# Block attention and a two-level Strassen feed-forward on one core: second-level weight sums one step later, two first loads on GpSimd's queue, a fifth raw weight tile, idle matmuls in two more places

## The chip, the core and the metric

One NeuronCore of a Trainium2 chip runs the whole program. Its engines work side by side and each runs its own instructions in order: TensorE (PE; its weight loads are the row PEld) multiplies, VectorE (DVE) and ScalarE (ACT) do elementwise work, GpSimd (POOL) and SyncE (SP) here mostly issue DMAs, as ScalarE does for a few. The metric is device time in microseconds (us), the median over runs of the program.

## What is computed

Attention with exponential decay, in blocks of 64 positions, and behind it a feed-forward layer. All in float32 at the output; the two weight matrices come as 64-bit floats and are rounded to float32 on the chip.

```python
batch, n_heads, seq, head_dim = (4, 8, 768, 64)
...
for b in range(nb):
    intra = np.einsum('bhic,bhjc->bhij', qb, kb) * Dmask[None]
    intra = np.einsum('bhij,bhjd->bhid', intra, vb)
    inter = np.einsum('bhid,bhde->bhie', qb * lam_pow[None], kv_state)
    out[:, :, sl] = intra + inter
    kv_state = lam_block[None, :, None, None] * kv_state + np.einsum('bhsd,bhse->bhde', kb_dec, vb)
...
x = attn_out.transpose(0, 2, 1, 3).reshape(B * S, H * D)   # 3072 x 512
h = x @ w_in                                               # 512 x 2048
g = h - np.tanh(h)
out = g @ w_out                                            # 2048 x 512
```

## The kernel before

**Groups and chunks.** The sequence is cut into six groups (g = 0 to 5) of 128 positions; a group over the four batch entries is 512 rows of x. A chunk is the part of one batch entry b in a group: its q, k and v, 256 KB each. So "the third chunk" is g=0, b=2, and "the fourth" is b=3.

**Attention of a chunk.** `att_transpose` puts q and k on their sides (for g 0 and 1 by TensorE, with ScalarE copying the result out of PSUM), `att_scores` makes the scores (matmuls L381 and L383 into `sp`, masked by VectorE in L387), `att_state` or `kv_products` the sum for the state (L401), `att_out` the output (L449, L459), copied to `xt` by ScalarE (L470).

**Loads.** `load_natural` loads q whole with one DMA, k and v with three: heads 0 to 3 whole (`whole_`, 128 KB), and heads 4 to 7 in two halves of 64 KB. For g=0 the halves of chunk 0 are issued by ScalarE, of the other chunks by GpSimd; the whole parts by SP, but for k of the second chunk (ScalarE). The program asks for q and k of chunks 0 and 1, v of these, q and k of chunk 2, the first block of w_in, q and k of chunk 3, v of chunks 2 and 3, and then further blocks of w_in. These issues are kept in program order on each queue.

**Weights.** w_in is cut into 16 blocks (`blocks`, u = 0 to 3 by i = 0 to 3), w_out into 16 (kt = 0 to 7, two each). A block arrives as 512 KB of 64-bit words in a tile `raw64`, of which there are `WAHEAD` = 4, used in turn; `weights(n)` rounds blocks up to the n-th, and asks for the load of blocks up to WAHEAD ahead. `round_block` rounds one: three ScalarE copies (L316 to L318) and two VectorE instructions (L320, L321). Most blocks are loaded by SP; the first four of w_out, numbers 16 to 19, by GpSimd. 

**Group 0** multiplies plainly with w_in (`up_plain`, matmuls L815 into `h`), with the last chunks' attention and the rounding of blocks between its steps. Group 1's attention is run beside the later units u.

**Group 0's second product** (`down_first`, matmuls L845 into seven PSUM tiles `acc`) walks over kt = 0 to 7 and uses Strassen's seven products. Its right factors are quarter matrices of w_out and sums of them: `pair[kt]` holds the two rounded blocks of kt, and `sums_out(kt)` makes the sums (L281 to L284) and stores them to DRAM with GpSimd's DMAs (`factors`, `fine`: L286, L287, L290). The tiles behind `pair` are used again after three steps: pair 3 lies where pair 0 was, pair 5 where pair 2 was, pair 7 where pair 4 was. In each step `sums_late` overwrites parts of g in place (L851, L852) after the products that read the old values; products n = 6 and 3 read the new ones. Steps 1 to 5 also round the two blocks of kt+2.

**Second-level sums.** Later groups use a second level of the same scheme, whose factors are again sums of sums. `sums_fine(u)` makes them from pairs 2u and 2u+1: four rounds (x = 5, 6, 7, 4) of two VectorE subtractions (L302, 128x128 and 128x512) into tiles `f`, each followed by a store to `fine` from GpSimd's queue (L304). The tiles `f` are those of k and v in the pool `io`; the four rounds of a pair take all four buffers of one size, so each L302 waits for the store of the same round of the pair before.

**Order.** Within an engine the scheduler of the language decides the order of instructions from the program's order and from when it reckons each can run; only what `keep_in_program_order` (or `tied(True, ...)`) marks keeps its order among marked instructions. Marked are the loads, all of attention for g=0, `sums_late`, the ScalarE roundings and L320 in the loop over kt, and L302 for u=0 alone.

**Idle matmuls.** At the start eight products of a tile of zeros (L340) run while the first q is on its way; their result is never read.

The loop over kt before:

```python
for kt in range(KH):
    if kt > 0:
        down_first(kt, (1, 2))
    sums_late(kt)
    if 0 < kt < KH - 2:
        weights(ready["done"] + 2)
        sums_out(kt + 2)
    down_first(kt, (5, 4, 7, 6, 3) if kt + 1 < KH else (5, 6, 7, 4, 3))
    if kt % 2 == 0:
        sums_fine(kt // 2)
```

Of the kernel before, what the change touches and what calls it, by code (L numbers as in the profile page):

```python
# [24 lines left out]
def kernel(  # L25
# [32 lines left out]
    nc = tc.nc  # L58
# [4 lines left out]
    KI = DM // 128  # L63
# [2 lines left out]
    HB = GRP // 2  # L66
    NU = DFF // 512
    KH = KO // 2
    WAHEAD = 4
    assert D == 64 and H * D == DM and KI == NP and B * S == NTOK  # L70
    assert S % BLK == 0 and B * BLK == GRP and DM == GRP == 512 and B == 4 and KI == 4

# [21 lines left out]
    fwd = const.tile([128, NP, BLK], F32)  # L94
# [7 lines left out]
    HALF = BLK // 2  # L102
# [26 lines left out]
    def tied(yes, op):  # L129
        return tc.keep_in_program_order(op) if yes else op  # L130
# [12 lines left out]
    def load_natural(g, b, names):  # L143
        for name, src, bufs in (("q", q, 2), ("k", k, 3), ("v", v, 4)):
            if name in names:
                if (g, b, name) in ((0, 2, "q"), (0, 3, "q"), (0, 3, "k")):
                    x = opool.tile([128, H, D], F32, name=f"{name}_nat", tag="o")
                else:
                    x = (qpool if name == "q" else io).tile([128, H, D], F32, name=f"{name}_nat", tag=name, bufs=bufs)
                rows = src[b, :, ts(g, BLK), :].rearrange("h s d -> s h d")  # L150
                if name == "q":
                    parts = [(nc.sync, x, rows)]
                else:
                    eng = nc.sync if g > 0 else nc.scalar if b == 0 else nc.gpsimd
                    whole_ = nc.scalar if (g, b, name) == (0, 1, "k") else nc.sync
                    parts = [(whole_, x[:, 0:4], rows[:, 0:4])] + [
                        (eng, x[ts(1 - t, HALF), 4:8], rows[ts(t, HALF), 4:8]) for t in range(2)]
                for eng, to, of in parts:
                    tc.keep_in_program_order(eng.dma_start(out=to, in_=of))
                raw[g, b][name] = x  # L160
# [58 lines left out]
    ready = {"loaded": 0, "done": 0}  # L219
# [8 lines left out]
    def load_block(eng, dst, kind, n, m, first=False):  # L228

        if kind == "out":  # L230
            tied(first, eng.dma_start(out=dst, in_=moe_w_out[ts(m * KH + n, 128), :].rearrange("k (a n) -> k a n", a=2)))
        elif m < 2:
            tied(first, eng.dma_start(out=dst, in_=w_in_u[ts(m, 128), :, ts(n, 256)]))
        else:
            for j in range(2):
                tied(first, eng.dma_start(out=dst[ts(1 - j, 64)], in_=w_in_u[ts(2 * m + j, 64), :, ts(n, 256)]))

    def load_weights(n):

        while ready["loaded"] < min(n, len(blocks)):  # L240
            if moe_w_in.dtype != F32:
                raw64 = stage.tile([128, 2, 256], I64, name="raw64", tag="raw64", bufs=WAHEAD)
                block = blocks[ready["loaded"]]
                load_block(nc.gpsimd if NU * KI <= ready["loaded"] < NU * KI + WAHEAD else nc.sync, raw64, *block, True)
                wraw[ready["loaded"]] = raw64
            ready["loaded"] += 1

    def weights(n):

        while ready["done"] < min(n, len(blocks)):  # L250
            at_ = ready["done"]
            load_weights(at_ + WAHEAD)
            kind, n_, m = blocks[at_]
            if kind == "out" and m == 0:
                pair[n_] = pair_tiles(n_)
            w = w1[n_][:, m] if kind == "in" else pair[n_][m][:, 0:2]
            if at_ in wraw:
                round_block(w, wraw.pop(at_), at_ < 2 * KI)
            else:
                load_block(nc.gpsimd, w, kind, n_, m)  # L260
            ready["done"] += 1

    def pair_tiles(kt):

        if kt % 3 == 2:
            x, y = (ws[u].rearrange("p x k c -> p (x k) c") for u in (3, 2))
            return x[:, 0:2], y[:, 0:6]
        wt = wst.tile([128, 8, 256], F32, name="wt", tag="w")
        return wt[:, 0:2], wt[:, 2:8]
# [23 lines left out]
    def sums_fine(u):  # L293

        (b11, b12), (b21, b22) = (tuple(pair[2 * u + i][1][:, 1:6, ts(j, 128)] for j in range(2)) for i in range(2))
        one = io.tile([128, 4, 1, 128], F32, name="f1", tag="k", bufs=3)
        parts = [(0, 1, [one[:, x] for x in range(4)]),
                 (1, 5, [io.tile([128, 4, 128], F32, name="f4", tag="v", bufs=4) for _ in range(4)])]
        for x, a, b in ((5, b12, b11), (6, b22, 5), (7, b22, b12), (4, b21, 6)):
            for lo, hi, t in parts:  # L300
                dst = {5: t[0], 6: t[1], 7: t[2], 4: t[3]}
                tied(u == 0, nc.vector.tensor_tensor(dst[x], a[:, lo:hi], dst[b] if isinstance(b, int) else b[:, lo:hi],  # L302
                                                     op=AL.subtract))
                nc.gpsimd.dma_start(out=fine[lo:hi, SUB.index(x), :, u, :].rearrange("n p c -> p n c"), in_=dst[x])  # L304
# [18 lines left out]
    def bank(name, tag, bufs):  # L323
        return psum.tile([128, 512], F32, name=name, tag=tag, bufs=bufs)
# [7 lines left out]
    for b, names in ((3, "qk"), (2, "v"), (3, "v")):  # L332
        load_natural(0, b, names)
    load_weights(WAHEAD)
    at["loaded"] = B


    idle = bank("idle", "w", 1)
    for _ in range(8):
        nc.tensor.matmul(out=idle[:, 0:128], lhsT=fwd[:, 0, :], rhs=fwd[:, 0, :], start=True, stop=True)  # L340


    state = const.tile([128, B, NP, D], F32)
# [4 lines left out]
    def att_transpose(g, bs):  # L348
        for b in bs:
            load(g * B + b + 1)  # L350
            t = raw[g, b]
            qt = work.tile([128, NP, BLK], F32, name="qt", tag="qt")
            kt = work.tile([128, NP, BLK], F32, name="kt", tag="kt")
            for dst, x in ((qt, "q"), (kt, "k")):
                if g >= GB:
                    tc.keep_in_program_order(nc.vector.transpose(out=dst.rearrange("d p i -> d (p i)"),
                                                                 in_=t[x + "b"].rearrange("d p r a -> d (p r a)")))
                else:
                    tp = bank("tp", "att", 4).rearrange("d (p s) -> d p s", p=NP)
                    for p in range(NP):  # L360
                        tied(g == 0 or p == 0, nc.tensor.transpose(out=tp[:, p, :], in_=t[x][:, 2 * p:2 * p + 2, :],
                                                                   identity=ident))
                    tied(g == 0, nc.scalar.activation(dst, tp, AF.Copy))
            qd = None
            if g > 0:
                qd = work.tile([128, NP, BLK], F32, name="qd", tag="qd")
                nc.vector.tensor_tensor(qd, qt, fwd, op=AL.mult)
            tr[g, b] = (qt, kt, qd)
# [21 lines left out]
    def att_decay(g, b):  # L390
        kp = raw[g, b]["k"].rearrange("s (p j) d -> s p j d", j=2)
        tied(g != 1, nc.vector.tensor_tensor(kp, kp, bwd, op=AL.mult))
# [13 lines left out]
    def att_state(g, bs):  # L406
        kv = kv_products(g, bs)
        tied(True, nc.scalar.activation(state[:, bs[0]:bs[0] + 2], kv, AF.Copy))
# [108 lines left out]
    def hidden(g, c):  # L517

        if (g, c) not in hid:
            hid[g, c] = gpool.tile([128, NU, 2, HB], F32, name=f"g{c}", tag=f"g{c}")  # L520
        return hid[g, c]
# [326 lines left out]
    def sums_late(kt):  # L848
        u, m = divmod(kt, 2)
        g11, g21, s1 = (hidden(0, c)[:, u, m] for c in (11, 21, "S1"))  # L850
        tc.keep_in_program_order(nc.vector.tensor_tensor(g11, s1, g11, op=AL.subtract))  # L851
        tc.keep_in_program_order(nc.vector.tensor_tensor(g21, g21, g11, op=AL.subtract))  # L852
# [27 lines left out]
    for b in (0, 1):  # L880
        att_transpose(0, (b,))
        att_decay(0, b)
        att_scores(0, (b,))
    att_state(0, (0, 1))
    att_transpose(0, (2,))
    att_out(0, (0, 1))
    unit = up_plain(0, by_rows(11, 21, 12, 22))
    att_decay(0, 2)
    att_scores(0, (2,))
    weights(1)  # L890
    att_transpose(0, (3,))
    att_decay(0, 3)
    steps(unit, 1)
# [12 lines left out]
    sums_first(0)  # L906
    load_weights(2 * KI + WAHEAD)
    p0, p1 = attention(1)
# [28 lines left out]
    for kt in range(KH):  # L937
        if kt > 0:
            down_first(kt, (1, 2))
        sums_late(kt)  # L940
        if 0 < kt < KH - 2:
            weights(ready["done"] + 2)
            sums_out(kt + 2)
        down_first(kt, (5, 4, 7, 6, 3) if kt + 1 < KH else (5, 6, 7, 4, 3))
        if kt % 2 == 0:
            sums_fine(kt // 2)
    first_results()
    sums_in(1)
    early.close()
# [120 lines left out]
```

## Time and profile before

| | us |
|---|---|
| median of 3 runs | 664.67 (662.13 to 666.44) |
| the profiled execution | 667.63 |
| its span, from first to last instruction | 665.7 |
| TensorE busy in the span | 649.9 |
| VectorE busy | 470.8 |
| ScalarE busy | 245.1 |
| GpSimd busy | 210.2 |
| mean granted clock of TensorE | 0.991 |

By stage (busy us of TensorE and VectorE, granted clock, share of time that the 16 DMA engines were busy):

| stretch of the span | what runs | TensorE | VectorE | clock | DMA |
|---|---|---|---|---|---|
| 0 to 15.4 | first loads, attention of chunks 0 and 1 | 10.23 | 6.90 | 1.00 | 1.02 |
| 15.4 to 30.6 | attention of chunks 2 and 3, first blocks | 12.78 | 5.39 | 0.78 | 0.98 |
| 30.6 to 107 | plain product with w_in, attention of group 1 | 76.32 | 57.33 | 1.00 | 0.80 |
| 107 to 140 | second product of group 0, kt 0 to 6 | 32.70 | 31.70 | 1.00 | 0.94 |
| 140 to 154 | kt 6 and 7, first results | 11.76 | 7.28 | 0.88 | 1.00 |
| 154 to 665.7 | groups 1 to 5 | 506.12 | 362.17 | 1.00 | 0.64 |

The profile has one execution. A group of instructions is named by its line, engine, operation and tiles; "out<-in" are the names of tiles. Times in it start at the first instruction. The DMA share is a mean over 16 engines and may read a little over 1. "Wait" is idle time of an engine, put down to the event that ended it. A product of float32 operands shows as two matmul records.

### The profile page before, as it was taken

What the parts mean: (1) busy time and instruction counts of PE and PEld (TensorE: products, weight loads), DVE (VectorE), ACT (ScalarE), POOL (GpSimd) and SP (SyncE); (2) the same over time, 40 slices, a digit from 0 to 9 for tenths busy, and PEclk for the clock granted to TensorE, in tenths of its full rate; (3) what the DMA queues carried; (4) which work ended last, traced back from release to release, by engine and by line L of the source; (5) the groups of instructions that cost most, each with busy time, mean ns of one, the idle gap of its engine ahead of it and who ended that gap; (6) DMA issues with size and microseconds to landing.
All of it is one profiled execution on the core that took longest, in us unless ns stands there. A gap on an engine that the chain in (4) does not pass through costs nothing.

```text
span 665.7 us, 14989 instructions
## 1 busy us (share of the span) xinstructions
PE 649.9 (98%) x5856; PEld 591.7 (89%) x5856; DVE 470.8 (71%) x889; ACT 245.1 (37%) x485; POOL 210.2 (32%) x363
## 2 busy tenths in 40 slices
PE   6899999989999999999999999999999999999998
PEld 5788888878888999988999988899998899998897
DVE  4366889956878794678885568896468877366933
ACT  3585865522331222532223442213453223363110
POOL 5000135694122455200344300254310155400251
PEclk9899999989999999999999999999999999999999
DMA  9859977999554777955586965387965277721395
GB/s 190 191 168 201 250 235 230 369 278 287 107 117 109 237 239 228 235 107 110 159 270 200 243 144 111 110 274 224 237 140 122 77 248 216 231 78 33 94 296 164
DMA packets 156549, 125.78 MB, mean 189 GB/s; under 512 B 128256, under 2 KB 129408, under 8 KB 156480
## 3 DMA queue, kind: packets, MB, share of 16 engines
q0 software_dynamic: 27168, 87.85, 42.8%
q1 hardware_dynamic: 127696, 36.60, 26.1%
q8 instruction: 46, 0.75, 0.5%
q10 hardware_dynamic: 1616, 0.39, 0.4%
q14 instruction: 23, 0.19, 0.1%
HBM read 103.81 MB, written 20.97 MB: 187 GB/s over the span
## 4 chain that ended last, share of the span: by engine, by line
PE 76%; issue 9%; DMA 6%; DVE 4%; ACT 2%; POOL 2%; ACTq 0%; SPq 0%; POOLq 0%; DVEq 0%
PE y L536 14%; PE y L762 11%; PE h L815 9%; PE zw L762 8%; PE z L536 5%; PE y L620 5%; PE w L708 4%; PE y L708 4%; PE z L620 3%; DMA k_nat<-in_k_dram 2%; PE sp L381 2%; PE acc L845 2%; DMA wb<-fine 2%; PE op L449 1%; DMA fine<-wt 1%
## 5 line engine op out<-in xcount | busy, mean ns | idle before, releaser
L670 POOL DMA_DIRECT2D wb<-fine x168 | 90.6, 540 | 205.4 <-PE y L708 83.0
L765 ACT ACTIVATE q<-y 128x128 f32<-128x128 f32 x96 | 26.6, 277 | 150.4 <-PE y L762 149.6
L815 PE MATMUL h<-xt,w 128*128 128x256 f32 x256 | 58.7, 387 | 2.5 <-DVE w L321 1.8
L762 PE MATMUL y<-wb,g 128*128 128x128 f32 x456 | 60.6, 278 | 0.0
L815 PEld LDWEIGHTS h<-xt,w 128*128 128x128 f32 x256 | 48.2, 192 | 10.2 <-DVE w L321 2.6
L762 PEld LDWEIGHTS y<-wb,g 128*128 128x128 f32 x456 | 55.1, 192 | 0.9
L673 POOL DMA_DIRECT2D wb<-factors x44 | 23.8, 542 | 86.4 <-PE y L708 49.0
L544 ACT ACTIVATE th<-g 128x512 f32<-128x512 f32 x40 | 25.2, 630 | 70.0 <-DVE g L562 53.6
L536 PE MATMUL y<-xt,w 128*128 128x256 f32 x192 | 45.0, 379 | 0.0
L545 DVE TENSOR_TENSOR g<-g,th 128x512 f32<-128x512 f32 x40 | 27.6, 691 | 20.7 <-ACT th L544 20.7
L762 PE MATMUL zw<-wb,g 128*128 128x128 f32 x304 | 40.3, 275 | 1.0 <-DVE g L767 1.0
L536 PEld LDWEIGHTS y<-xt,w 128*128 128x128 f32 x192 | 36.4, 190 | 5.1 <-ACT g L553 0.2
L536 PE MATMUL y<-tt,ws 128*128 128x256 f32 x160 | 38.5, 379 | 0.0
L845 PE MATMUL acc<-wt,g 128*128 128x256 f32 x144 | 35.6, 397 | 2.5 <-DVE g L852 2.0
L536 PE MATMUL y<-tt,w 128*128 128x256 f32 x160 | 38.1, 381 | 0.0
L536 PE MATMUL z<-xt,ws 128*128 128x256 f32 x160 | 38.1, 381 | 0.0
L762 PEld LDWEIGHTS zw<-wb,g 128*128 128x128 f32 x304 | 37.0, 192 | 1.2 <-DVE g L767 1.2
L708 PE MATMUL y<-wb,g 128*128 128x256 f32 x160 | 37.3, 379 | 0.0
L708 PE MATMUL w<-wb,g 128*128 128x256 f32 x160 | 35.5, 380 | 0.0
L845 PEld LDWEIGHTS acc<-wt,g 128*128 128x128 f32 x144 | 27.8, 196 | 8.4 <-DVE g L852 2.4
L708 PEld LDWEIGHTS y<-wb,g 128*128 128x128 f32 x160 | 30.4, 190 | 4.1
L708 PEld LDWEIGHTS w<-wb,g 128*128 128x128 f32 x160 | 30.3, 190 | 4.2
(197 smaller groups left out, 1455.2 us busy)
## 6 DMA issues: line engine op xcount, KB each, us to landing
wb<-fine POOLq DMA_DIRECT2D x168, 256.0 KB, 3.6
wb<-factors POOLq DMA_DIRECT2D x44, 256.0 KB, 4.3
wb<-fine_in POOLq DMA_DIRECT2D x36, 256.0 KB, 4.0
raw<-in_moe_w_out_dram SPq DMA_DIRECT2D x12, 512.0 KB, 5.6
raw<-in_moe_w_in_dram SPq DMA_DIRECT2D x8, 512.0 KB, 5.8
raw<-in_moe_w_in_dram SPq DMA_DIRECT2D x16, 256.0 KB, 5.7
fine<-f POOLq DMA_DIRECT2D x16, 256.0 KB, 5.2
q_blk<-in_q_dram SPq DMA_DIRECT2D x128, 32.0 KB, 3.1
```

Source lines behind the costliest of these rows:

```text
L381: tied(g == 0, nc.tensor.matmul(out=sp[j][ts(r, HALF), x:3 + p:2 + p - x, :], lhsT=k0, rhs=qj.rearrange("d (t i) -> d t i", t=2), start=Tr ...
L536: nc.tensor.matmul(out=t[:, m, :], lhsT=wt[:, kt, ts(m, 128)], rhs=x[:, kt, :], start=first and m == 0 and kt == 0, stop=kt == 1, skip_gro ...
L544: nc.scalar.activation(th, src, AF.Tanh)
L545: nc.vector.tensor_tensor(dst(c), src, th, op=AL.subtract)
L620: nc.tensor.matmul(out=dst[:, ts(u, 128)], lhsT=a, rhs=b, start=x in (1, 2, 5) and u == 0, stop=True, skip_group_check=True)
L670: nc.gpsimd.dma_start(out=t.rearrange("p m c -> p (m c)"), in_=fine[TWICE.index(n_), SUB.index(x_)].rearrange("p u c -> p (u c)"))
L673: nc.gpsimd.dma_start(out=t, in_=factors[XAT[FACT[n_][1]]][:, 2 * x_:2 * x_ + 2, :])
L708: nc.tensor.matmul(out=t[:, m, :], lhsT=a[:, u, kt, ts(m, 128)], rhs=wb[:, kt, :], start=first and u == 0 and m == 0 and kt == 0, stop=u = ...
L762: nc.tensor.matmul(out=dst, lhsT=a[:, u, :], rhs=wb[:, ts(u, 128)], start=x in (1, 2) and u == 0, stop=u == NU - 1, skip_group_check=True)
L765: nc.scalar.activation(keep, dst, AF.Copy)
L815: tied(u == 0, nc.tensor.matmul(out=hm[c][:, m, :], lhsT=w1[u][:, i, a, ts(m, 128)], rhs=xt[0, t][:, i, :], start=m == 0 and i == 0, stop= ...
L845: nc.tensor.matmul(out=acc[n][:, r, :], lhsT=a[:, ts(r, 128)], rhs=b, start=kt == 0 and r == 0, stop=kt == KH - 1, skip_group_check=True)
```

## The change

Five edits.

1. `WAHEAD` goes from 4 to 5: there are five tiles `raw64`, and each block of weights is asked for one block earlier. Blocks 16 to 19 stay on GpSimd's queue.
2. The first block of w_in (number 0) is loaded through GpSimd's queue in place of SP's.
3. The whole part of the third chunk's k is loaded through GpSimd's queue, after its two halves, in place of SP's. For all other loads the order stays.
4. The idle matmuls become a function: seven at the start in place of eight, four more after the state products of chunks 0 and 1, six more before the transposes of the fourth chunk. They are kept in program order.
5. In the loop over kt, `sums_fine(u)` moves from the end of step kt=2u to step 2u+1, behind its `sums_late` and ahead of its `weights`.

```diff
-    WAHEAD = 4
+    WAHEAD = 5
...
-                    whole_ = nc.scalar if (g, b, name) == (0, 1, "k") else nc.sync
-                    parts = [(whole_, x[:, 0:4], rows[:, 0:4])] + [
-                        (eng, x[ts(1 - t, HALF), 4:8], rows[ts(t, HALF), 4:8]) for t in range(2)]
+                    whole_ = {(0, 1, "k"): nc.scalar, (0, 2, "k"): nc.gpsimd}.get((g, b, name), nc.sync)
+                    parts = [(eng, x[ts(1 - t, HALF), 4:8], rows[ts(t, HALF), 4:8]) for t in range(2)]
+                    parts.insert(2 * (whole_ is nc.gpsimd), (whole_, x[:, 0:4], rows[:, 0:4]))
...
-                load_block(nc.gpsimd if NU * KI <= ready["loaded"] < NU * KI + WAHEAD else nc.sync, raw64, *block, True)
+                load_block(nc.gpsimd if ready["loaded"] in (0, *range(NU * KI, NU * KI + 4)) else nc.sync, raw64, *block, True)
...
-    for _ in range(8):
-        nc.tensor.matmul(out=idle[:, 0:128], lhsT=fwd[:, 0, :], rhs=fwd[:, 0, :], start=True, stop=True)
+    def warm(n):
+        for _ in range(n):
+            tc.keep_in_program_order(nc.tensor.matmul(out=idle[:, 0:128], lhsT=fwd[:, 0, :], rhs=fwd[:, 0, :], start=True,
+                                                      stop=True))
+    warm(7)
...
     att_state(0, (0, 1))
+    warm(4)
     att_transpose(0, (2,))
     att_out(0, (0, 1))
...
     weights(1)
+    warm(6)
     att_transpose(0, (3,))
...
         sums_late(kt)
+        if kt % 2 == 1:
+            sums_fine(kt // 2)
         if 0 < kt < KH - 2:
             weights(ready["done"] + 2)
             sums_out(kt + 2)
         down_first(kt, (5, 4, 7, 6, 3) if kt + 1 < KH else (5, 6, 7, 4, 3))
-        if kt % 2 == 0:
-            sums_fine(kt // 2)
```

## The prediction

> **What bounds the kernel now.** I read first the page's busy shares and forty slices, then TensorE's waits and its order of time, then the granted clock in short stretches, then VectorE and GpSimd at the one long wait, last the DMA queues.
>
> ```profile
> PE 649.9 (98%) x5856; PEld 591.7 (89%) x5856; DVE 470.8 (71%) x889; ACT 245.1 (37%) x485; POOL 210.2 (32%) x363
> PE   6899999989999999999999999999999999999998
> PEclk9899999989999999999999999999999999999999
> ```
> TensorE is the bound nearly everywhere. It is short of work or of clock in two places: the first two slices (0 to 33 us) and the ninth (133 to 150 us). From 30.7 to 107 it is busy 76.32 of 76.40 us, and after 154 it is busy 506.12 of 511.7 us. So a microsecond won before 30.7 or near 144 should reach the end.
>
> The start, from TensorE's order of time (start, duration, then in brackets the idle time and who ended it):
> ```profile
> 13.78 0.63 PE L361 MATMUL tp<-ident,q_nat 128*128 128x128 f32 x4 [1.40 <-DMA q_nat<-in_q_dram]
> 15.43 0.63 PE L361 MATMUL tp<-ident,k_nat 128*128 128x128 f32 x4 [1.02 <-DMA k_nat<-in_k_dram]
> 22.75 1.95 PE L815 MATMUL h<-xt,w 128*128 128x256 f32 x4 [1.77 <-DVE w L321]
> 30.68 1.56 PE L815 MATMUL h<-xt,w 128*128 128x256 f32 x6 [0.70 <-ACT xt L470]
> ```
> Waits: q of the third chunk, k of the third chunk, the first rounded w_in block, the second half of x. Now the clock (stretch, its length, busy time and count of the five engine rows; the third number from the end is the granted clock, then DMA share and GB/s):
> ```profile
> 12.60:16.00 3.40, 1.20 (x10) 0.85 (x10) 0.00 (x0) 1.01 (x2) 0.00 (x0) 1.00 1.14 241
> 16.00:19.40 3.40, 3.40 (x81) 3.28 (x84) 0.69 (x1) 0.96 (x2) 0.00 (x0) 0.51 1.23 198
> 19.40:22.85 3.45, 1.68 (x33) 1.37 (x27) 2.20 (x5) 3.45 (x8) 0.00 (x0) 0.99 0.99 261
> 22.85:26.25 3.40, 3.40 (x37) 2.44 (x37) 0.46 (x2) 1.94 (x4) 0.00 (x0) 0.51 1.07 233
> ```
> A stretch of 3.4 us in which TensorE was busy 1.20 us is followed by one at half clock; so is the stretch with 1.68 us busy. Stretches with more work keep the clock. The DMA share is about 1 throughout: the start is bound by bytes too.
>
> The ninth slice, VectorE, GpSimd and TensorE in order of time:
> ```profile
> 138.50 2.60 POOL L304 DMA_DIRECT2D fine<-f  x4
> ...
> 140.54 0.69 DVE L302 TENSOR_TENSOR f<-wt,f 128x512 f32<-128x512 f32 x1 [1.70 <-DMA fine<-f]
> ...
> 143.68 0.69 DVE L302 TENSOR_TENSOR f<-wt 128x512 f32<-128x512 f32 x1 [1.91 <-DMA fine<-f]
> 144.29 0.42 DVE L852 TENSOR_TENSOR g<-g,g 128x256 f32<-128x256 f32 x1
> ...
> 144.76 4.51 PE L845 MATMUL acc<-wt,g 128*128 128x256 f32 x12 [2.01 <-DVE g L852]
> ```
> The late sum L852 of kt=6 stands in VectorE's queue behind a second-level sum L302 of the last pair, which waits until the store of the pair before has left its tile f. TensorE waits 0.23 us for L851 and 2.01 us for L852, then runs twelve matmul records in 4.51 us.
>
> Two answers on DMA queues for 2 us, from 72 to 74, where GpSimd loads raw blocks of 512 KB beside SP's loads (packets, MB, share of time):
> ```profile
> q0 software_dynamic: 116, 0.45, 80.8%
> q1 hardware_dynamic: 392, 0.09, 30.1%
> ```
> GpSimd's queue (q0) then takes 225 GB/s and leaves SP's (q1) 45.
>
> **The change part by part.** The sum is made against the profiled execution, 667.63 us; the median of the three runs is 664.67, so 2.96 is taken off at the end.
>
> *Third chunk's k.* SP issues one 128 KB DMA fewer; GpSimd issues it after the two halves of this k, at about 6.1 us, and k of the fourth chunk and all v halves queue behind it. Before, it was issued at 6.46 and landed 8.8 us later, at 15.3. GpSimd's two halves for the fourth chunk, the same bytes at the same place in its queue, landed at 13.3 and 14.4. So k should be there at about 14.4, when the transposes of q end (13.78 + 0.63): the 1.02 us wait goes. Bounds: 0 to 1.02; taken 1.0. q stays on SP and still ends its own wait near 13.7.
>
> *First w_in block.* GpSimd issues it at about 6.8, SP at 9.26 before (landing 17.46). It lies in q0 behind the k halves and that k, so it starts near 14 and, at the 225 GB/s above, takes 2.3 us: about 17, as before. What moves is what stands behind: k halves of the fourth chunk come after it on GpSimd's queue, but q and k of that chunk are earlier on SP's. By bytes (1 MB for chunks three and four's k and q, w the same, v last) the fourth k lands 0 to 1.2 us before its 19.8 (issued 10.86, 8.9 to landing); taken 0.3. SP's issue times are hidden (it stands idle later); GpSimd's 0.6 us each too.
>
> *Idle products.* Eight take 3.78 us at the start, 0.47 each at half clock; at full clock I estimate 0.23 from L815, where sixteen records with twice the columns take 3.65 us (two records a product). One fewer at the start frees 0.47 us in which only later landings wait: 0. Four after the first state products: 0.9 us inside the 1.40 us wait for q, cost 0 (0.5 over if at half clock, 1.9). Six before the fourth chunk's transposes: 1.4 us, inside the wait for the fourth k, cost 0 (up to 1.4 if at half clock, 2.8).
>
> *What the start then looks like.* Stretch 12.6 to 16.0 gets 1.2 + 0.65 of idle products + about 1.0 of op products (which start at 15.0): near 2.9 of 3.4 us busy, so I take full clock after it. The 3.4 us at 0.51 shrink to 1.7. Chunk three's work ends near 17.3, six idle products near 18.7, then the transposes wait for the fourth k until 19.5 (19.89 before): so of 1.0 + 1.7 only 0.4 comes through here. But ScalarE copies x near 16.5 to 17.5 and rounds the first block from 17.5 (20.00 before), L321 is done by 20.2, and L815 starts at 20.6, after the transposes, in place of 22.75: 2.1 won. If the second stretch at half clock (22.85 to 26.25) goes as well, 1.7 more: 3.8. If neither clock holds, the path is 0.9 better at most. Taken 3.0, between 2.1 and 3.8; bounds 0 and 3.8. Later weights keep up: the second block lands near 23 and is needed after x's second half.
>
> *Fifth raw tile.* Each load of a block can start one block earlier; SP waits 27.9 us in nine waits on ScalarE's rounding in the whole run and 16.2 in three more on its first copies. In the middle ScalarE waits only 0.7 and 0.5 us for raw blocks, off the path: 0 there. In the down stage it takes up to 512 KB out of the crowded stretch 107 to 131, where stores of sums land after 8 to 9 us (5 elsewhere).
>
> *Second-level sums.* No instruction is added. Sums of pair u go from the end of kt=2u behind L851 and L852 of kt=2u+1. VectorE issues eight L302 a pair, 0.28 to 0.69 each; GpSimd's eight stores keep their place before the next pair's factors. On the path: 0.23 + 2.01 of waits, and the clock after them: twelve records in 4.51 us against 0.22 each gives about 1.7. Sum 3.9. Bounds: 0 (only pair 0's sums are tied to program order, and the trace has L302 of later pairs pulled ahead) and 3.9. I take 3.9, since the moved sums have lower priority and the raw loads leave the stores' way. The place of the eight L302 is hidden: VectorE is idle 1.84 and 1.28 us around the last late sums. Next late would be the second late sum of kt=7 or the first results, with 1 to 2 us to spare.
>
> *Sum.* 667.63 - 3.0 - 3.9 = 660.7; less 2.96, **657.8 us**.
>
> **Rivals.** *The wait moves and stays* (0.20). L302 is free to be pulled into any gap, and the stores of the pair before still land late (POOL is busy issuing from 131.2 to 149). Against: less DMA traffic before. 664.7 - 3.0 = 661.7.
>
> *The start gives nothing* (0.14). The bytes are the same, the share of 16 engines is 1, and the fourth k ends the wait anyway; the clock falls as before since phases of the 3.4 us stretches are not set by the kernel. 664.7 - 3.9 - 0.3 = 660.5. The Trainium skill, DMA: Bandwidth & Descriptors, section "Issuing engines are not separate DMA queues", says that another issuer saves only issue time; by that rule moving k and w is worth nothing, though the 72 to 74 rows show shares move with the queue. The Trainium skill, TensorE: Matmul & The Clock Gate, Part 1, lets the clock drop after at least one idle window of about 3.4 us; by it gaps of 1.0 to 1.8 us would cost no clock and idle products nothing would win, but here 1.20 and 1.68 us busy of 3.4 were not enough.
>
> *Neither* (0.08): the order is the same in effect and the start too: 664.5.
>
> *Slower: pair tiles come free too late* (0.12). L302 of pair u must read before the tile of pair tile 2u is rounded into again. If L302 with x=7 truly waits for L852 of kt=2u+1, it moves from 119.91 to past 123.4 for u=1, 3.5 us; ScalarE's L316 follows it directly (120.27), and the sums of that tile (done 127.3) would be 3.5 later at 130.9, just where its first matmuls stand (130.87). For u=0 the room is 2.4 us (116.0 to 118.46), for u=2 4.4. Past about 2.4 to 3.5 us each pair brings a wait like the one above, 2.0 + 1.7. Three of them, less the start: 664.7 + 11.1 - 3.0 = 672.8; two: 669.1. Against: L302 of the next pair was pulled ahead by more than a kt in this trace.
>
> **How the numbers follow.** The forecast has 0.46 (its own range 655.5 to 660.5). The range must hold it and the three middle rivals and may leave out most of the slower one: 654.5 to 667, with run scatter of about 2 us (662.13 to 666.44). A change over 1% is 6.6 us, about what a measurement of this kernel can tell. Faster by more (under 658.0): 0.65 of the forecast's 0.46 and a little of the others, 0.33. Slower by more (over 671.3): two thirds of 0.12, 0.09 with a remainder. Within: 0.58.
>
> **What would show it.** k's wait near 15.4 gone; PEclk near 1 from 16 to 26; L815's first wait under 0.5 us; TensorE running on from about 27.7 us in place of 30.68; no wait of L302 between L851 and L852, and no stretch at 0.67 near 145. Wrong would be: q of the third chunk later than 14.5, idle products at 0.47 each, the fourth chunk's transposes past 20.5, or TensorE waiting for a pair tile at kt=3, 5 or 7.

## The result, and the profile after

| | before | changed |
|---|---|---|
| median, 15 runs each (us) | 664.76 (661.64 to 668.98) | 667.74 (666.06 to 672.14) |
| the profiled execution (us) | 667.63 | 668.86 |
| its span (us) | 665.7 | 666.8 |

The ratio of the changed kernel to the one before, by the means of the runs, is 1.0057, 95% interval 1.0034 to 1.008: slower by 3.8 us (2.3 to 5.3); the medians differ by 3.0. That is under the 1% that the prediction named as about what a measurement can tell, but it is clear of the scatter, and the sign is the other one: 657.8 was forecast, with a range up to 667.

The page of the changed kernel, busy shares and the two TensorE rows of the forty slices:

```profile
PE 648.6 (97%) x5874; PEld 591.3 (89%) x5874; DVE 471.0 (71%) x889; ACT 245.4 (37%) x485; POOL 211.8 (32%) x365
PE   7789999989999999999999999999999999999998
PEclk9899999999999999999999999999999999999999
```

TensorE is still the bound. The hole in the first two slices and the one in the ninth are both still there, and a small one in the third (8, where it was 9) has come.

The start, from TensorE's order of time (start, duration, count, then idle time and who ended it; lines behind the idle products have moved by six):

```profile
12.98 1.16 PE L343 MATMUL idle<-fwd 128*128 128x128 f32 x8
13.97 0.60 PE L367 MATMUL tp<-ident,q_nat 128*128 128x128 f32 x4
14.41 0.60 PE L367 MATMUL tp<-ident,k_nat 128*128 128x128 f32 x4
...
20.98 0.27 PE L389 MATMUL sp<-qt,kt 64*64 64x64 f32 x1 [3.93 <-issue]
21.68 2.93 PE L343 MATMUL idle<-fwd 128*128 128x128 f32 x12
24.40 0.92 PE L367 MATMUL tp<-ident,q_nat 128*128 128x128 f32 x4
...
32.23 1.13 PE L821 MATMUL h<-xt,w 128*128 128x256 f32 x4 [0.70 <-ACT xt L476]
```

The wait for k is gone (14.41 follows 13.97 without a bracket). But in the middle of the third chunk's scores TensorE now stops for 3.93 us for which the profile names no event ("issue"), then runs six idle products at half clock, 2.93 us, before the fourth chunk's transposes. The long run of w_in products starts at 32.23, where it was 30.68.

The clock there, in the stretches shown before (length, busy time and count per engine, then granted clock, DMA share, GB/s):

```profile
16.00:19.40 3.40, 1.05 (x47) 0.78 (x43) 0.00 (x0) 2.63 (x5) 0.00 (x0) 1.00 1.26 216
19.40:22.85 3.45, 1.87 (x26) 1.71 (x27) 1.23 (x3) 0.27 (x1) 0.00 (x0) 0.82 1.07 249
22.85:26.25 3.40, 3.40 (x21) 3.31 (x19) 1.28 (x3) 0.84 (x2) 0.00 (x0) 0.68 1.06 227
```

The full clock from 16.00 was kept as forecast, and was spent on standing still: 1.05 us of 3.40 busy.

A wait that before did not have, at 45 us. ScalarE of the changed kernel, ScalarE of the one before, then TensorE of the changed one, each in order of time:

```profile
41.14 0.67 ACT L316 ACTIVATE w<-raw 128x512 f32<-128x512 f32 x1 [1.16 <-DMA raw<-in_moe_w_in_dram]
42.04 0.60 ACT L826 ACTIVATE th<-h 128x512 f32<-128x512 f32 x1 [0.22 <-PE h L821]
44.96 0.67 ACT L316 ACTIVATE w<-raw 128x512 f32<-128x512 f32 x1 [2.33 <-DMA raw<-in_moe_w_in_dram]
45.53 1.06 ACT L826 ACTIVATE th<-h 128x512 f32<-128x512 f32 x2
```

```profile
42.21 0.60 ACT L820 ACTIVATE th<-h 128x512 f32<-128x512 f32 x1 [0.27 <-PE h L815]
42.70 0.67 ACT L316 ACTIVATE w<-raw 128x512 f32<-128x512 f32 x1
```

```profile
46.88 2.86 PE L821 MATMUL h<-xt,w 128*128 128x256 f32 x12 [1.43 <-DVE g L827]
50.16 17.62 PE L821 MATMUL h<-xt,w 128*128 128x256 f32 x80 [0.42 <-DVE w L321]
```

In the changed kernel ScalarE stands in two roundings (L316) whose loads have not landed, with a tanh (L826) queued behind each. Before, the first of these roundings came behind the third tanh (42.21) and did not wait. VectorE's g = h - tanh(h) (L827) waits for the tanh, and TensorE waits for it to free its PSUM tile.

The ninth slice, VectorE and TensorE:

```profile
145.03 0.42 DVE L857 TENSOR_TENSOR g<-gS,g 128x256 f32<-128x256 f32 x1
145.36 0.28 DVE L302 TENSOR_TENSOR f<-wt 128x128 f32<-128x128 f32 x1
147.36 0.69 DVE L302 TENSOR_TENSOR f<-wt 128x512 f32<-128x512 f32 x1 [1.72 <-DMA fine<-f]
147.97 0.42 DVE L858 TENSOR_TENSOR g<-g,g 128x256 f32<-128x256 f32 x1
```

```profile
148.44 2.86 PE L851 MATMUL acc<-wt,g 128*128 128x256 f32 x12 [1.81 <-DVE g L858]
```

The same picture as before the change: a second-level sum stands between the two late sums of kt=6, waiting 1.72 us for a store, and TensorE waits 1.81 us (2.01 before). Only the half clock behind it is missing this time: twelve records take 2.86 us, where it was 4.51.

### The profile page after: what moved, and what is told of

Its sections match the earlier page's. It is cut to its first block, busy times and chain, and to the rows that moved or that the text cites. A ratio compares the mean times of both kernels' runs of the same rounds, so it can differ in the third digit from the quotient of the medians.

```text
span 666.8 us, 15013 instructions
## 1 busy us (share of the span) xinstructions
PE 648.6 (97%) x5874; PEld 591.3 (89%) x5874; DVE 471.0 (71%) x889; ACT 245.4 (37%) x485; POOL 211.8 (32%) x365
## 3 DMA queue, kind: packets, MB, share of 16 engines
q1 hardware_dynamic: 126896, 35.94, 25.5%
## 4 chain that ended last, share of the span: by engine, by line
PE 79%; DVE 6%; ACT 5%; DMA 4%; issue 3%; POOL 1%; SPq 1%; DVEq 0%; ACTq 0%; POOLq 0%
PE y L542 17%; PE y L768 11%; PE zw L768 8%; PE z L542 6%; PE y L626 6%; PE w L714 5%; PE y L714 5%; PE h L821 5%; PE z L626 3%; DMA v_nat<-in_v_dram 2%; PE sp L387 2%; PE op L455 1%; PE op L431 1%; PE acc L851 1%; PE w L626 1%
## 5 line engine op out<-in xcount | busy, mean ns | idle before, releaser
L851 PE MATMUL acc<-wt,g 128*128 128x256 f32 x144 | 33.5, 382 | 2.2 <-DVE g L858 1.8
L542 PEld LDWEIGHTS z<-xt,ws 128*128 128x128 f32 x160 | 30.2, 190 | 4.2
```

The lines of the kernel that those rows point to most:

```text
L542: nc.tensor.matmul(out=t[:, m, :], lhsT=wt[:, kt, ts(m, 128)], rhs=x[:, kt, :], start=first and m == 0 and kt == 0, stop=kt == 1, skip_gro ...
L851: nc.tensor.matmul(out=acc[n][:, r, :], lhsT=a[:, ts(r, 128)], rhs=b, start=kt == 0 and r == 0, stop=kt == KH - 1, skip_group_check=True)
```

## The experiments

Twelve kernels in three sets of four, each timed in twelve runs beside the kernel before on the same chip (its medians were 664.46, 665.32 and 665.22). Ratios are to the kernel before.

| kernel | what it is | ratio | 95% interval |
|---|---|---|---|
| sums_only | before + moved sums | 1.0019 | 0.9998 to 1.004 |
| ahead_only | before + fifth raw tile | 1.0033 | 1.001 to 1.0056 |
| queue_only | before + the two loads on GpSimd's queue | 1.0007 | 0.9985 to 1.0028 |
| idle_only | before + idle products 7, 4, 6 | 1.0007 | 0.9986 to 1.0028 |
| sums_tied | sums_only, last pair's sums held to order | 0.9973 | 0.9946 to 1.0001 |
| ahead_order | ahead_only, two roundings held behind tanhs | 0.9988 | 0.9956 to 1.0019 |
| no_idle | before without any idle product | 0.9988 | 0.996 to 1.0017 |
| after_4tiles | changed kernel with four raw tiles | 1.0015 | 0.9988 to 1.0042 |
| before_tied | before, last pair's sums held to order | 0.9944 | 0.9927 to 0.9961 |
| tied_again | sums_tied once more | 0.9961 | 0.9945 to 0.9977 |
| tied_queue | sums_tied + queue_only | 0.9978 | 0.9959 to 0.9996 |
| all_mended | the whole change, both orders held | 0.9987 | 0.9965 to 1.0008 |

**The four parts alone.** Each takes one edit of the change (the last takes the whole edit 4).

> The kernel before with the second-level sums moved and nothing else. Theory A (the loss comes from the start and from the fifth raw tile; the moved sums only shift a wait): TensorE still waits 1.5 to 2.3 us for the second late sum of kt=6 behind an L302 that waits for a store, time 664.8 -1 to +1. Rival B (the moved sums are what costs, because pair tiles come free later): waits of TensorE on pair tiles or late sums grow by 2 us or more, time +2 to +4. The prediction's step: the waits near 144 and the half clock after them gone, -3.9.

> The kernel before with five raw tiles in place of four, blocks 16 to 19 still on GpSimd's queue. Theory A: the scheduler puts two roundings of blocks of the third unit ahead of the first tanhs on ScalarE, they wait 1 to 2.5 us for their loads, TensorE waits 1 to 2 us for a PSUM tile near 43 to 47 us: +1 to +2. Rival (the wait at 46.9 of the changed kernel only comes from its late start): no such wait here, 0 +-0.7. The prediction's step: 0 in the middle, stores a little earlier after 107, 0 to -1.

> The kernel before with the third chunk's whole k and the first w_in block on GpSimd's queue, no other edit. Theory A (what costs at the start is that TensorE reaches code that is not loaded yet): TensorE still runs 16 to 19.4 at half clock and gets there late enough, no stop over 1 us for 'issue', the k wait gone, long product from 30 to 31, -1 to +0.5. Rival C (the GpSimd block starves SP's queue and the code loads): a stop of 2 us or more near 17 to 21 for 'issue' or for the fourth chunk's q or k, +1.5 to +3.

> The kernel before with idle matmuls 7, 4 and 6 in place of 8, 0 and 0. Theory A: full clock from 16 on, TensorE reaches the third chunk's scores near 17.5, stops 1 to 2 us for 'issue', and the six idle matmuls (1.4 to 2.8 us) lie on the path: long product from 30 to 32 us, -0.5 to +1.5. Rival C (idle matmuls are harmless, the GpSimd block costs): no stop, long product from 27.5 to 29.5, -1 to -3.

None shows a gain, and only the fifth tile's loss is clear of zero by itself. The four excesses add to 0.66%, the whole change measured 0.57%: within intervals of about 0.2% on each, the loss is the sum of its parts, and about half of it is the fifth tile, which the prediction had at nothing. In ahead_only's trace the wait of the changed kernel is there at the same place, 1.08 us on g and 0.42 us on a rounded block; sums_only keeps a wait of 1.6 us on L852. queue_only loses the wait for k and meets the stop, here 2.42 us: its Theory A, no stop over 1 us, was wrong; Rival C had the stop, but most of its +1.5 to +3 us lies outside the interval (-1.0 to +1.9). idle_only went as its Theory A in kind, with a stop of 2.35 us and the six idle products on the path, though its long run started at 29.01 and not between 30 and 32. The order of time on TensorE in queue_only:

```profile
12.85 0.63 PE L361 MATMUL tp<-ident,q_nat 128*128 128x128 f32 x4 [0.63 <-DMA q_nat<-in_q_dram]
13.37 0.63 PE L361 MATMUL tp<-ident,k_nat 128*128 128x128 f32 x4
...
18.56 0.32 PE L381 MATMUL sp<-qt,kt 64*64 64x128 f32 x1 [2.42 <-issue]
```

The third chunk's transposes of k start 2.06 us earlier than in the trace of before (13.37 against 15.43; in sums_only, with the loads of before, they start at 14.64, so part of this is the draw of one execution), and the long run of products starts at 30.54, only 0.14 us earlier. Nor do the moved loads and the idle products win together: after_4tiles, which has both and the moved sums, is at 1.0015, sums_only at 1.0019, the same within their intervals.

**The fifth tile: is it the order on ScalarE?** ahead_order keeps the fifth tile and holds the roundings of w_in blocks 8 and 9 behind the third and fourth tanh, by an order without a wait.

```diff
-    WAHEAD = 4
+    WAHEAD = 5
...
-        tied(first or ready["done"] >= NU * KI, nc.scalar.activation(w, hif, AF.Copy, scale=2.0 ** -112))
+        op = tied(first or ready["done"] >= NU * KI, nc.scalar.activation(w, hif, AF.Copy, scale=2.0 ** -112))
+        if ready["done"] in (8, 9):
+            tc.add_manual_dep(op.ins, tanhs[ready["done"] - 6].ins.name, mybir.DependencyInfo(
+                mybir.DependencyClass.NoSync, mybir.DependencyReason.DATA), reason="order")
...
-                nc.scalar.activation(th, hm[c], AF.Tanh)
+                tanhs.append(nc.scalar.activation(th, hm[c], AF.Tanh))
```

> Five raw tiles, with the roundings of blocks 8 and 9 held behind the third and fourth tanh of the first unit on ScalarE, as they stood before. Theory A (the fifth tile costs by the order on ScalarE): no wait of TensorE for L821 of 1 us or more between 38 and 50, time 664.5 +-1.2. Rival (the fifth tile costs by DMA traffic or space): the loss of ahead_only stays, 666.5 to 668.

> The changed kernel with four raw tiles in place of five. Theory A (parts add: five tiles +2.2, sums +1.3, the rest 0): 665 to 666.5, no wait for L827 near 46.9. Rival (the start with both its edits is what costs in the changed kernel): 667 to 668.5, as the changed kernel.

ScalarE and TensorE of ahead_order in order of time (L316 is L318 here, and later lines have moved by five):

```profile
42.71 0.60 ACT L825 ACTIVATE th<-h 128x512 f32<-128x512 f32 x1 [0.27 <-PE h L820]
43.21 0.67 ACT L318 ACTIVATE w<-raw 128x512 f32<-128x512 f32 x1
43.77 0.59 ACT L825 ACTIVATE th<-h 128x512 f32<-128x512 f32 x1
44.25 0.68 ACT L318 ACTIVATE w<-raw 128x512 f32<-128x512 f32 x1
```

```profile
31.18 29.13 PE L820 MATMUL h<-xt,w 128*128 128x256 f32 x132 [0.70 <-ACT xt L475]
```

With the tanhs ahead, the roundings find their blocks landed and TensorE runs 132 records without a gap. The ratio falls from 1.0033 to 0.9988. Taking the fifth tile out of the changed kernel instead moves it from 1.0057 to 1.0015. Both say 0.4%, near 3 us, each with an interval of about 0.4% either way. Of that, the traces locate 1.5 us (ahead_only) and 1.9 us (changed) in the waits named; the rest is not placed in any one trace. With the order held, neither harm nor gain of the tile itself can be measured. The harm is that the rounding stands ahead of the tanh, while in the changed kernel the two loads land 4.8 and 6.7 us after their issue. Why it stands there, that with one more buffer the scheduler reckons the block ready earlier, is argued and not shown.

**The sums: is it the place of the call or the order on VectorE?** sums_tied is sums_only with one more word: the L302 of the last pair keep program order, as those of u=0 do. before_tied is that word alone, with the sums where the kernel before has them.

```diff
-                tied(u == 0, nc.vector.tensor_tensor(dst[x],
+                tied(u in (0, 3), nc.vector.tensor_tensor(dst[x],
```

> The kernel before with the second-level sums moved, and those of the last pair also held to program order, so that no L302 of u=3 stands before the late sums of kt=6 and 7 on VectorE. Theory A (the prediction's price was right, the edit did not do it because the scheduler pulls L302 ahead): no wait of TensorE over 0.5 us between 135 and 150, no half clock there, 1.5 to 4 us below sums_only: 662.5 to 665. Rival (the stores or pair tiles bound this stretch anyway): the wait comes back at the first results or the next product, within 1 us of sums_only (666.65).

> The kernel before with the second-level sums where it has them; only the sums of the last pair (u=3) are held to program order on VectorE, so that none of its L302 stands between the late sums L851 and L852 of kt=6. Theory (the wait is cured by the order on VectorE, and the place of the call in the code has nothing to do with it): no wait of TensorE on L852 over 0.5 us, about 2 us of waits gone, so 0.3% under the kernel before, as sums_tied had it (0.9973). Rival (the moved call is what pays, or the two together): the wait at kt=6 goes but another of 1 to 2 us comes in its place, ratio 0.999 to 1.001.

> sums_tied a second time, for its interval, beside the same runs as the others: sums moved and the last pair held to order. Theory: 0.9973 again within 0.002, no L852 wait, TensorE without a gap from 140 to 154 us. Rival (the first measurement was favoured by the draw of the start): 0.999 or above.

VectorE and TensorE of before_tied around kt=6 and 7:

```profile
138.75 0.42 DVE L851 TENSOR_TENSOR g<-gS,g 128x256 f32<-128x256 f32 x1
139.27 0.42 DVE L852 TENSOR_TENSOR g<-g,g 128x256 f32<-128x256 f32 x1
139.61 0.89 DVE L302 TENSOR_TENSOR f<-wt 128x128 f32<-128x128 f32 x2
...
143.30 0.69 DVE L302 TENSOR_TENSOR f<-wt 128x512 f32<-128x512 f32 x1 [1.52 <-DMA fine<-f]
...
145.25 0.42 DVE L851 TENSOR_TENSOR g<-gS,g 128x256 f32<-128x256 f32 x1
145.77 0.43 DVE L852 TENSOR_TENSOR g<-g,g 128x256 f32<-128x256 f32 x1
```

```profile
139.56 5.34 PE L845 MATMUL acc<-wt,g 128*128 128x256 f32 x24
144.74 1.03 PE L845 MATMUL acc<-wt,gS 128*128 128x256 f32 x4
145.72 3.72 PE L845 MATMUL acc<-wt,g 128*128 128x256 f32 x16
```

L851 and L852 of kt=6 now stand together. A sum still waits 1.52 us for a store at 143.30, but no late sum that TensorE waits for is held by it: TensorE runs through 139.56 to 149.3 without a gap. This kernel has the lowest ratio of the study, 0.56% or 3.7 us (2.6 to 4.9) under the one before, and it has none of the change's five edits. Theory and rival are both answered by four kernels (call moved or not, order held or not): the order on VectorE is the cure, and the moved call does not help it. With the sums moved as well (tied_again, beside the same runs) the gain is 0.39%. The difference of 0.17% is within the two intervals, but it is what sums_only lost too (0.19%), and the traces show something for it: all seven kernels with moved sums have a wait of 0.47 to 0.64 us on L851 of kt=2, between 114 and 121 us, and none of the seven traces without the move has it. In tied_again:

```profile
114.19 1.99 PE L845 MATMUL acc<-ws,g 128*128 128x256 f32 x8 [0.50 <-DVE g L851]
```

The eight L302 of pair 0, about 3.3 us of VectorE, now stand between the late sums of kt=1 and of kt=2.

Not all of the 3.7 us is placed. Nine traces have the wait at kt=6: 1.1 to 2.2 us on L852 (mean 1.57), 0.30 in the mean on L851, and half clock behind it in two of the nine (4.51 and 4.54 us for twelve records, 2.86 in the others). That makes 2.2 us in the mean, just under the low end of the interval.

**The start.** Is the stop tied to the idle products, or to a place in TensorE's program? no_idle has no idle product at all.

> The kernel before with no idle matmuls at all. Theory code (the stop for 'issue' is a block of TensorE's code that arrives late, at a fixed place of its instruction stream: 17 matmul records into the third chunk's scores with eight products ahead of it, 11 with eleven): with none it moves 16 records on, to the fourth chunk's transposes, where TensorE waits for loads anyway; the first chunks run at half clock, and time is 664.5 -1.5 to +1. Rival (the stop comes from a semaphore or from the queue at that place of the program): it stays inside the third chunk's scores, or none is seen, +1 to +3 for the cold start.

The stop moved with the program. With the eight idle products of before it falls 17 records into the 32 of the third chunk's scores (queue_only, sums_only). With eleven ahead, three products or six records more, it falls after 11 records (idle_only, after_4tiles). With none it falls behind all 32, at the fourth chunk's transposes:

```profile
21.28 0.60 PE L358 MATMUL tp<-ident,q_nat 128*128 128x128 f32 x4 [2.05 <-issue]
```

It fits a fixed place counted in instructions, the end of a piece of TensorE's program. The DMA queues show what may be the piece. In the changed kernel between 17.5 and 18 us (packets, MB, share of 16 engines):

```profile
q1 hardware_dynamic: 140, 0.03, 57.2%
q0 software_dynamic: 29, 0.04, 41.8%
q8 instruction: 1, 0.02, 17.1%
```

One packet on the queue of instructions, among data that fill the engines. It has about 16 KB: the page of the changed kernel counts 47 packets and 0.77 MB on this queue. All the kernels with the stop, in order of the time at which TensorE comes to it:

| kernel | TensorE reaches the place | packet seen in the half us from | TensorE goes on | stop | long run of w_in products from |
|---|---|---|---|---|---|
| queue_only | 16.14 | 15.5 | 18.56 | 2.42 | 30.54 |
| tied_queue | 16.21 | 15.5 | 18.67 | 2.46 | 30.14 |
| after_4tiles | 16.33 | 16.0 | 18.83 | 2.50 | 29.77 |
| all_mended | 16.79 | 18.0 | 21.51 | 4.72 | 33.27 |
| changed | 17.05 | 17.5 | 20.98 | 3.93 | 32.23 |
| idle_only | 17.36 | 17.0 | 19.71 | 2.35 | 29.01 |
| sums_tied | 17.46 | 15.5 | 18.23 | 0.77 | 29.39 |
| sums_only | 17.47 | 17.5 | 20.77 | 3.30 | 33.01 |
| tied_again | 17.50 | 15.0 | 18.00 | 0.50 | 27.59 |
| before_tied | 17.56 | 16.5 | 19.56 | 2.00 | 30.73 |
| ahead_order | 17.73 | 16.5 | 19.42 | 1.69 | 31.18 |
| no_idle | 19.23 | 18.5 | 21.28 | 2.05 | 29.66 |

In all twelve TensorE goes on 2.7 to 3.5 us after the start of the half microsecond that shows the packet, whatever the time at which it came to the place. In the traces of before and ahead_only the packet is at 15.5 and 14.5 and no stop is seen there; their long run starts at 30.68 and 27.15. In the trace of before TensorE came to this place only near 19.4, at half clock, and 15.5 plus 2.7 to 3.5 is earlier.

A second stop of the same kind supports this reading. In after_4tiles, in the fourth chunk's outputs:

```profile
27.64 0.81 PE L455 MATMUL op<-ss,v_nat 128*64 128x64 f32 x21 [1.45 <-issue]
```

The next packet of that queue is in the half us from 24.5, 3.1 us before. no_idle (packet from 25.5, restart 28.48, stop 0.76) and the changed kernel (27.5, 30.11, 0.16) have it too, 3.0 and 2.6 us after their packets; the other eleven traces show none. From the first place to the second there are 124 matmul records in after_4tiles and in the changed kernel, with twelve idle ones among them, and 125 in no_idle, with none.

So the start of these kernels goes with the time of the first packet. In the seven traces in which TensorE's program up to there is that of before (before, sums_only, ahead_only, sums_tied, before_tied, tied_again, ahead_order) the packet is seen from 14.5 to 17.5, and the long run starts between 27.15 (ahead_only, the earliest packet) and 33.01 (sums_only, the latest), mean 29.96; in the six with an edit that should bring it forward between 29.01 and 33.27, mean 30.83. The stop in those six is 3.06 us in the mean, in the seven 1.18: TensorE comes earlier and stands longer.

**Together.**

> sums_tied and the two loads on GpSimd's queue (third chunk's k, first w_in block), no idle products between chunks, four raw tiles. Theory (the queue's gain of 1 us is eaten by the stop for code at the third chunk's scores): as sums_tied, ratio 0.996 to 0.999. Rival (the queue's gain adds once the ninth slice is mended): 1 us less than sums_tied, 0.995 to 0.996.

> The whole change with both mends: the roundings of w_in blocks 8 and 9 held behind the third and fourth tanh on ScalarE, and the sums of the last pair held to order on VectorE. Theory (the loss of the change is the fifth tile's order and the sums' order, and the start gives nothing): 3.8 us less than the changed kernel at 1.0057 of the one before, minus what the wait at kt=6 cost before: ratio 0.996 to 0.999, no wait on g between 38 and 50 us nor between 140 and 154. Rival (the start edits lose in sum, by idle products at half clock and the stop for code): 1.000 to 1.003 with both waits gone.

all_mended is the whole change with the two orders held. It has neither wait (TensorE runs 122 records of w_in products in 26.97 us without a gap, and is busy 14.00 of 14.00 us from 140 to 154), and goes from 1.0057 to 0.9987: the two orders are worth about 0.7%, 4.7 us, in the changed kernel, with an interval of about 2 us either way. Even so its ratio does not come to that of before_tied, nor do those of tied_queue and tied_again, though tied_again's interval overlaps. Its profiled start was the worst of the study, from TensorE's order of time:

```profile
21.51 0.37 PE L394 MATMUL sp<-qt,kt 64*64 64x64 f32 x1 [4.72 <-issue]
...
22.76 2.93 PE L348 MATMUL idle<-fwd 128*128 128x128 f32 x12
```

The best version found is before_tied, 661.35 us where the kernel before beside it has 665.22.

## Why the prediction was wrong, point by point

**Third chunk's k, first block, idle products: -3.0 us forecast, no gain measured.** The steps up to 17 us hold: k's wait gone, the stretch from 16.00 at full clock, eight idle records in 1.16 us at full clock and without a gap behind them. The step that failed is "L815 starts at 20.6", and with it "TensorE running on from about 27.7": the profile has 25.59 and 32.23. It took every instruction as there when its operands are. By the reading above, the code of the rest of the third chunk's scores comes by DMA among the same saturated transfers, and in the twelve traces TensorE goes on with it only at 18.0 to 21.5 us. A microsecond won ahead of that place is stood out at it: the wait went from k to code. Nothing in the trace of before shows that stop: it was one of the two executions in which the packet came early enough to cause none. The rival "the start gives nothing", at 0.14, had this part's result, but for other reasons (bytes, the fourth k, the clock).

**Idle products hidden: "cost 0" failed for the six.** They stand behind the stop and not inside the wait for the fourth k, which has by then landed; they are on the path with 1.60 us (idle_only, after_4tiles) or 2.93 us (the changed kernel, all_mended). Against that stands the clock: with them and a stop of 2.35 or 2.50 us the next two stretches stay at 1.00, where sums_only, queue_only, tied_queue and before_tied, without them and with stops of 2.0 to 3.3 us, go to 0.50 to 0.67. With a stop of 3.93 or 4.72 us the clock fell in spite of them, and no_idle, with none and a stop of 2.05 us, kept it. In sum, 1.0007; and no_idle, at 0.9988 (0.996 to 1.0017), says that the idle products of before win nothing that can be measured either.

**Fifth raw tile: "0 there" failed.** The prediction looked for the effect in when loads start and found room. It did not ask what else could change with the number of buffers: here the order on ScalarE. Measured: about 0.33% alone, 2.2 us (0.7 to 3.7).

**Second-level sums: -3.9 us forecast, +0.19% measured.** The step that failed is that the move removes the wait ("since the moved sums have lower priority"): in the changed kernel L302 of the last pair still stands between the late sums of kt=6, and TensorE waits 1.81 us. Where the wait is gone, in before_tied, the gain is 3.7 us, near the 3.9 of the forecast; but the traces place only 2.2 us of it, so that the sizes agree is partly luck. The prediction named its own doubt, that only pair 0's sums are held to program order, and gave it 0.20 under "the wait moves and stays"; that rival is what happened, at the same place, with the same instructions. The prediction also put 1.7 us of half clock to the wait's account, which came in two of nine traces with the wait: that term was a draw of one execution. The rival "pair tiles come free too late" did not happen: no trace with moved sums has a wait of over 0.5 us at kt=3, 5 or 7.

**The sum.** 6.9 us of gain were forecast and 3.8 of loss came, 10.7 apart. Both terms of the forecast failed, which is its rival "neither", at 0.08 and 664.5 us; that rival too left out what the fifth tile costs. The parts account for it: the sums 3.9 and about 1.3, the start 3.0 and about 0.9, the fifth tile 2.2, together 11.3, with intervals of 1.5 us on each measured part.

**Queues and code.** The Trainium skill, DMA: Bandwidth & Descriptors, "Issuing engines are not separate DMA queues", says that another issuer saves only the time of the issue; by it, moving the loads would be worth nothing. The time came out so, but not by that rule: the queue did change what landed when. In the microsecond from 12 to 13 the changed kernel's queues moved this (packets, MB, share):

```profile
q0 software_dynamic: 75, 0.26, 97.0%
q1 hardware_dynamic: 27, 0.01, 4.2%
```

Before, the same microsecond had 0.09 MB on GpSimd's queue (q0) and 0.08 MB on SP's (q1). The Trainium skill, Runtime: NRT & Kernel Launch, "Instruction fetch mechanics", has instructions fetched in blocks of 16 KiB while the block before is executed, the crossing "mostly hidden". The block size agrees with the packet (0.77 MB in 47 packets); the hiding does not here: stops of 0.50 to 4.72 us in twelve of the fourteen traces.

## What to carry to other kernels

When a wait is behind one in-order queue, look at who stands in front of the late instruction and hold that order itself; moving the call in the source may leave that order as it was, and giving a buffer more may change the order on another engine. Where transfers fill the DMA engines, the program's own code can, as it seems here, come late too, so a microsecond won on data ahead of the next piece of code may be lost at it. One profile of a start that varies by 6 us between traces with the same TensorE program up to there can't size an edit of 1 us; the timed runs bound it to about 0.2%.

## What the runs showed of the hardware

The stop for code was not expected: a 16 KB packet, 2.7 to 3.5 us from its half microsecond to the restart, in stretches with a DMA share of 1.0 to 1.3. That the packet is TensorE's is inferred from that nearly constant distance, from the place moving with the count of instructions, and from the second stop 124 or 125 records on; the profile doesn't name the engine. Whether the loads on GpSimd's queue make it later is open: the packet was seen at 15.9 us in the mean of the seven traces with TensorE's program of before and at 16.6 in the six with some edit of the start, and it varies by 2.5 to 3 us in each.

The clock did not follow busy time in a stretch alone. A stretch with 1.57 us busy of 3.45 was followed by one at 1.00 (no_idle), one with 1.46 of 3.40 by one at 0.52 (sums_only); with six idle products behind the stop 0.90 was followed by 1.00 (after_4tiles) and 0.78 by 0.58 (all_mended). The limits of these stretches are chosen by hand; where the clock's own lie was not measured, so what decides stays open.
